# A planned attention stage: copies out of shared PSUM banks enter the operation order, fewer and larger loads, one longer warming

## The chip, the cores and the metric

One core of one Trainium2 chip. The metric is the device time of one execution in microseconds; the median of three executions stands for the kernel.

## The reference

Causal attention with a forget bias on 4 batches of 8 heads (576 positions, head size 64, float32), and behind it two feed-forward blocks on the 2304 x 512 result. Per head, `c` is the running sum of `max(s, 0)` and

```
scores = q @ k.T / 8 + min(c[j] - c[i], 0)      (j > i: -1e9)
attn   = exp(scores - rowmax);  attn /= sum(attn) + 1e-9;  x = attn @ v
x = (sigmoid(x @ w_gate) * (x @ w_val)) @ w_out        (512 -> 1536 -> 512)
h = x @ w_in;  out = (h * cos(h)) @ w_out2             (512 -> 2048 -> 512)
```

The weights arrive as 64-bit floats and are decoded on the chip into a high and a low float32 part; a product of the blocks takes three matmuls (high x high, high x low, low x high).

## The kernel before, in words

The attention works on 16 pairs of heads. Its operations carry short names with the pair's number last. For pair p: `GQ`, `GK` load Q and K (512 of the 576 rows, one DMA per head; the last 64 rows of all 8 heads of a batch come by `GQT`, `GKT`), `GV` loads V (one DMA per head with all 576 rows, the fifth chunk filled up with 64 rows of the next head), `DB` spreads the running sums over the partitions (pair 0 does it with matmuls `B0`, `B1` instead, and copies `BC`), `PQ`, `PK` transpose Q and K with TensorE, `HQ`, `HK` copy them out of PSUM, `A4`, `A5`, `A3`, `A2`, `A0` are the score matmuls of the query blocks, `ZT`, `ZA`, `ZM`, `Z` mask the bias on GpSimd, `X` is the biased row minimum on VectorE (L662), `E` the exponential on ScalarE (L666), `T` the transposes of the weights back into PSUM (L444), `C` their copies into the SBUF tile `pt` (L433 on ScalarE, L437 on VectorE), `V0`, `V1` the product with V (L736, L738), `U` its copy to `w`, and `RA RC RT RR RD RB M XH XL` form the reciprocals of the sums (RA on GpSimd L745, RC on VectorE L748), turn them, store them to DRAM (RD), spread them back into `rb` (RB, L762), multiply (`M`, L768) and split the result in high and low parts.

The two `T` of one query-block group (blocks 0 and 1, or the two heads of block 2 or of block 3) write into one pair of PSUM banks, and two `C` copies empty it. Where these two copies go to different engines, the program makes the second wait for the first, since both read the same banks.

The order of all this is a list, `SEQ`, of about 1,100 names (the suffix `:a`, `:d` or `:p` gives ScalarE, VectorE or GpSimd). Every engine, and SyncE that issues the loads, works through its own part of the list strictly in order. `Plan.run` goes through the list with planned durations only to hand out buffers and PSUM banks. The list was made outside the kernel with the same plan. Behind the attention, `I0` to `I7` are the first up-projection of the first feed-forward block, and from `moe()` on the blocks follow; `glu` (L835 to L844) is their first gate, on ScalarE and VectorE.

At the start TensorE runs six matmuls on zeros (L453), six 256-column matmuls as warming (`warm0`, L495), `B0` and `B1` on 32 rows (L569), the first transposes (L552), and six more warming matmuls (`warm1`) ahead of the first scores (L626, L631).

Of the kernel before, what the change touches and what calls it, by code (L numbers as in the profile page):

```python
# [10 lines left out]
F32 = mybir.dt.float32  # L11
# [72 lines left out]
class Op:  # L84
    __slots__ = ("name", "alts", "fn", "deps", "ready", "bufs", "out", "unit", "start", "end", "n", "xfer", "mode")
# [5 lines left out]
SWITCH = 0.15  # L91


class Plan:
# [3 lines left out]
    def op(self, name, alts, rd=(), wr=(), needs=(), xfer=0.0, at=0.0):  # L98
        o = Op()
        o.name, o.alts, o.xfer = name, alts, xfer  # L100
# [25 lines left out]
    def run(self, seq):  # L126
# [3 lines left out]
        for word in seq.split():  # L130
# [32 lines left out]
WARM = 2  # L163
# [31 lines left out]
C1.2.8:d E1.1.9 w0mant_hi E0.1.9 A2.9 E1.3.9 U7:d Z0.10:p C0.4.8:a T0.1.9 RB6 T0.0.9 C0.0.9:a RC8 A5.9 ZM0.3.10 T0.3.9 T1.3.9 C0.1.9:a GK13 X0.2.9 GV8 X1.2.9 Z1.10:p
E1.2.9 C1.3.9:a X0.4.9 PQ11 ZT1.10 PK11 ZT0.10 A3.10 ZM1.3.10 GQT12 ZA1.10 ZA0.10 HK11:a C0.3.9:d HQ11:d GQ12 A4.10 RT8 A0.10 E0.4.9 M6:p X1.3.10 XH5:p X0.3.10 RR8:a
# [23 lines left out]
def kernel(  # L220
# [14 lines left out]
    B, H, S, D = q.shape  # L235
# [153 lines left out]
    def attention():  # L389
        with ExitStack() as c2:  # L390
# [79 lines left out]
            def setup_tail(u):  # L470
# [6 lines left out]
                for i in range(NV):  # L477
                    u.memset(VN[i][TAIL:P, NT4], 0.0)
# [592 lines left out]
```

## Time and profile before

| | us |
|---|---|
| median of 3 executions | 1038.0 |
| lowest, highest | 1037.33, 1042.3 |
| the profiled execution | 1042.41 |
| its span (first to last instruction) | 1040.6 |
| TensorE busy in it | 1014.0 |
| VectorE, ScalarE, GpSimd busy | 704.6, 477.9, 410.4 |

Busy times are sums over instructions; TensorE's are modelled, so that a stretch that is called busy is not one at its peak. Idle times stand in brackets behind an instruction with what ended them.

### The profile page before, as it was taken

Reading aid. Unit: us, or ns where it says so; the run is one execution under the profiler, and the core shown is the slowest. Engines: PE = TensorE matmul, PEld = TensorE weight load, DVE = VectorE, ACT = ScalarE, POOL = GpSimd, SP = SyncE. Lnnn points to the kernel's source line nnn. Section 1 sums busy time; section 2 is a strip of 40 time slices with the busy share of each in tenths; the row PEclk is TensorE's granted clock in tenths of the full one; section 3 lists DMA queues with packets and bytes.
Section 4 is the critical chain, followed back from the end, with each engine's and each line's share of the span. In section 5 each row is a group of like instructions: output and inputs, shape, how many; then the busy total and the mean of one; then the engine's idle time right before and its main releaser. Section 6 shows DMA issues by size and latency. Waiting matters only on the chain.

```text
span 1040.6 us, 17428 instructions
## 1 busy us (share of the span) xinstructions
PE 1014.0 (97%) x6554; PEld 917.6 (88%) x6554; DVE 704.6 (68%) x1366; ACT 477.9 (46%) x1079; POOL 410.4 (39%) x489
## 2 busy tenths in 40 slices
PE   9999897899999999999999999999999999999998
PEld 5665555799999999999999999999999999999997
DVE  5777875565655557644334888888688878886565
ACT  5888885342222222222121335666555455554443
POOL 4456885341222223321111234555255535552222
PEclk9999999999999999999999999999999999999999
DMA  7778763221111112111010112122011201200111
GB/s 175 182 183 194 186 156 81 93 82 41 41 41 41 61 42 61 62 43 39 21 42 21 41 61 61 41 61 61 1 61 42 60 22 41 62 1 13 49 61 61
DMA packets 93956, 69.94 MB, mean 67 GB/s; under 512 B 61296, under 2 KB 82160, under 8 KB 93872
## 3 DMA queue, kind: packets, MB, share of 16 engines
q1 hardware_dynamic: 92224, 68.37, 23.1%
q8 instruction: 51, 0.84, 0.3%
q10 hardware_dynamic: 1648, 0.47, 0.2%
q14 instruction: 33, 0.27, 0.1%
HBM read 63.95 MB, written 4.87 MB: 66 GB/s over the span
## 4 chain that ended last, share of the span: by engine, by line
PE 81%; DVE 0%; ACT 0%; issue 0%; DVEq 0%; ACTq 0%
PE pw L356 21%; PE pw L357 21%; PE pw L355 21%; PE pw L918 6%; PE pw L919 6%; PE pw L920 6%; DVE acc L936 0%; DVE gl L844 0%; ACT gh L838 0%; ACT tm L835 0%; DVEq L1066 0%; ACTq L838 0%
## 5 line engine op out<-in xcount | busy, mean ns | idle before, releaser
L355 PE MATMUL pw<-XH,wp 128*128 128x384 f32 x960 | 323.1, 337 | 1.0 <-DVE w L437 1.0
L356 PE MATMUL pw<-XL,wp 128*128 128x384 f32 x960 | 323.0, 336 | 0.0
L357 PE MATMUL pw<-XH,wp 128*128 128x384 f32 x960 | 322.9, 336 | 0.0
L310 POOL TENSOR_TENSOR wp<-wm,wp 128x512 fp32r<-128x512 f32 x68 | 101.4, 1491 | 228.6 <-DVE wp L309 228.0
L355 PEld LDWEIGHTS pw<-XH,wp 128*128 128x128 f32 x960 | 180.4, 188 | 4.8 <-DVE w L437 1.1
L356 PEld LDWEIGHTS pw<-XL,wp 128*128 128x128 f32 x960 | 180.3, 188 | 3.6
L357 PEld LDWEIGHTS pw<-XH,wp 128*128 128x128 f32 x960 | 180.3, 188 | 0.0
L908 POOL TENSOR_TENSOR gl<-tm,gh 128x384 fp32r<-128x384 f32 x96 | 108.9, 1135 | 142.7 <-ACT gh L907 142.6
L302 POOL TENSOR_TENSOR wm<-wm,wx 128x512 int32<-128x512 int32 x68 | 90.5, 1331 | 181.8 <-DVE wm L301 177.3
L836 DVE TENSOR_TENSOR tm<-pw,tm 128x384 f32<-128x384 f32 x72 | 40.1, 557 | 154.2 <-PE pw L357 139.6
L918 PE MATMUL pw<-wp,gh 128*128 128x512 f32 x288 | 112.2, 389 | 0.0
L919 PE MATMUL pw<-wp,gh 128*128 128x512 f32 x288 | 112.1, 389 | 0.0
L920 PE MATMUL pw<-wp,gl 128*128 128x512 f32 x288 | 112.0, 389 | 0.0
L838 ACT CAST gh<-tm 128x384 fp32r<-128x384 f32 x72 | 37.0, 514 | 140.7 <-DVE tm L836 139.9
L893 DVE SCALAR_TENSOR_TENSOR tm<-tm 128x384 f32<-128x384 int32 x96 | 99.1, 1032 | 3.3
L894 ACT ACTIVATE tm<-tm 128x384 f32<-128x384 f32 x96 | 50.5, 527 | 108.9 <-DVE tm L893 108.9
L355 PE MATMUL pw<-gh,wp 128*128 128x384 f32 x288 | 97.0, 337 | 2.3 <-ACT gh L838 2.3
L356 PE MATMUL pw<-gl,wp 128*128 128x384 f32 x288 | 97.3, 338 | 0.2 <-DVE gl L844 0.2
L357 PE MATMUL pw<-gh,wp 128*128 128x384 f32 x288 | 96.7, 336 | 0.0
L289 ACT ACTIVATE wx<-wx,ebias 128x512 int32<-128x512 int32 x68 | 49.2, 723 | 100.3 <-DVE wx L288 99.3
L666 ACT ACTIVATE pu<-pu,nm 128x576 f32<-128x576 f32 (+4 forms) x144 | 83.3, 581 | 5.4 <-DVE nm L662 5.4
L901 DVE SCALAR_TENSOR_TENSOR tm<-tm,pw 128x384 f32<-128x384 f32 x96 | 52.8, 550 | 42.4 <-ACT tm L895 42.4
(100 smaller groups left out, 1621.4 us busy)
## 6 DMA issues: line engine op xcount, KB each, us to landing
raw<-in_moe_w_out_dram SPq DMA_DIRECT2D x28, 512.0 KB
CB<-cum_d SPq DMA_DIRECT2D x15, 576.0 KB
raw<-in_moe_w_in_dram SPq DMA_DIRECT2D x16, 512.0 KB
raw<-in_moe_w_gate_dram SPq DMA_DIRECT2D x12, 512.0 KB
raw<-in_moe_w_val_dram SPq DMA_DIRECT2D x12, 512.0 KB
VN<-in_v_dram SPq DMA_DIRECT2D x31, 160.0 KB
rb<-rec_d SPq DMA_DIRECT2D x32, 144.0 KB
out_dram<-acc SPq DMA_DIRECT2D x17, 256.0 KB
```

What stands on the lines that cost most here:

```text
L302: pool.tensor_tensor(m, m, st["x"], ALU.add)
L310: pool.tensor_tensor(w[:, 1], m, f(w[:, 0]), ALU.subtract)
L355: pe.matmul(ps, wh, xh, start=first, stop=False)
L356: pe.matmul(ps, wh, xl, start=False, stop=False)
L357: pe.matmul(ps, wl, xh, start=False, stop=last)
L666: act.activation(o, o, AF.Exp, bias=NMT[nm.slot][:, col:col + 1], scale=-1.0, accum_out=SUMS[sums.slot][:, col:col + 1])
L893: dve.scalar_tensor_tensor(r, kk, -TWO_PI_LO, r, ALU.mult, ALU.add)
L901: dve.scalar_tensor_tensor(g, r, -0.5, h, ALU.add, ALU.mult)
L908: pool.tensor_tensor(gl, g, f(gh), ALU.subtract)
L918: pe.matmul(ps, gh[:, ts], w[:, 0], start=it["first"], stop=False)
L919: pe.matmul(ps, gh[:, ts], w[:, 1], start=False, stop=False)
L920: pe.matmul(ps, gl[:, ts], w[:, 0], start=False, stop=it["last"])
```

## The change

The list is new as a whole. The plan that goes with it knows that a copy waits for all transposes and copies ahead of it in its banks; some planned durations differ. Q and K of a pair come in one DMA each, V's fifth chunk comes once per batch into a tile of its own (`vt`), the warming is one operation of 11 matmuls and `warm1` is gone, and `B0`, `B1` read all 128 rows of a tile that VectorE has set to zero first.

```diff
-    def op(self, name, alts, rd=(), wr=(), needs=(), xfer=0.0, at=0.0):
+    def op(self, name, alts, rd=(), wr=(), needs=(), xfer=0.0, at=0.0, ser=None):
...
+            if o.ser:
+                b, copy = o.ser
+                s = max(s, b.turned if copy else 0.0, b.copied + LAT[b.unit] if b.unit not in (None, u) else 0.0)
...
-WARM = 2
+WARM = 11
...
-tail cum GQ0 warm0 GKT0 B1 B0 GQT0 PQ0 table GK0 out BC0:a BC1:a GQ1 ZT0.0 PK0 GK1 warm1 Z0.0:p HQ0:a ZT1.0 Z1.0:p DB1 ZM0.3.0 PQ1 ZA0.0 HK0:d A3.0 ZM1.3.0 ZA1.0 X0.3.0
...
-X1.1.14 E0.3.14 T0.4.13 X1.0.14 V0.12 X0.0.14 X0.1.14 E0.2.13 E1.0.14 E1.1.14 XL9:p RC12 DB15 V1.12 M11:p E0.1.14 C0.4.13:d RT12 A2.14 U12:d RA13 E0.0.14 RR12:a ZM0.2.14
-E1.3.14 T0.1.14 RC13 ZT0.15 RD12 X0.2.14 T0.0.14 Z0.15:p C0.0.14:d XL10:p T0.2.13 C0.1.14:a Z1.15:p T1.2.13 A5.14 E0.2.14 T0.3.14 X1.2.14 RB12 ZM0.3.15 T1.3.14 X0.4.14
...
-w2split U14:a C0.4.15:d V0.15 XH13:d M14:d RD15 XH14:d XL14:p RB15 V1.15 U15:d XL13:d M15:p XH15:a XL15:p
+warm0 GQ0 tail cum table GKT0 GK0 GQT0 B0 BC0:d PK0 PQ0 Z0.0:p B1 out HQ0:a BC1:a ZT0.0 GK1 HK0:d A4.0 ZA0.0 GQ1 A0.0 X0.1.0 Z1.0:a PK1 DB1 ZT1.0 A3.0 GQ2 ZA1.0 X0.0.0
...
+X1.0.15 E0.2.14 RD12 E0.1.15 M11:d XH11:p E0.0.15 E1.0.15 T0.1.14 E1.1.15 U13:d T0.0.14 C0.0.14:a A5.14 ZM0.3.15 RB12 T0.1.15 RA13 T0.0.15 X0.4.14 C0.1.14:a w1split A5.15
...
+T0.4.14 T0.4.15 XH12:p C0.4.15:d RB13 XL12:p w2exponent I5 I6 RC15 I7 XL11:d RD14 T0.2.15 M13:d C0.4.14:a w2mant_hi RT15 T1.2.15 C0.3.15:a C0.2.15:a V0.14 w2mant_lo
+RR15:a V1.14 U14:d RD15 w2sign RB14 C1.2.15:a M14:d RB15 w2split V0.15 XH13:p XL13:p V1.15 XH14:a U15:d M15:d XL14:p XH15:d XL15:d
...
-            VN = [att.tile([P, NQ, 2, D], F32, name=f"VN{i}") for i in range(NV)]
+            VN = [att.tile([P, NT4, 2, D], F32, name=f"VN{i}") for i in range(NV)]
+            VT = [att.tile([P, PB, 2, D], F32, name=f"vt{i}") for i in range(2)]
...
+            dve.memset(WT[1], 0.0)
...
-            for i in range(WARM):
+            for i in range(1):
...
-                    for z in range(6):
-                        pe.matmul(PW[:, wm.slot, 0:2 * P], one_b[:, 0:P], one_b, start=z == 0, stop=z == 5)
...
+                    for z in range(WARM):
+                        pe.matmul(PW[:, wm.slot, 0:2 * P], one_b[:, 0:P], one_b, start=z == 0, stop=z == WARM - 1)
...
-                        for e in range(2):
-                            u.dma_start(out=QKN[x][qk.slot][:, :, e], in_=src[e, 0:NT4 * P].rearrange("(p c) d -> p c d", c=NT4))
+                        u.dma_start(out=QKN[x][qk.slot], in_=src[:, 0:NT4 * P].rearrange("e (p c) d -> p c e d", c=NT4))
...
-                                pe.matmul(PW[:, bs.slot + z, 0:HS], ident[0:NH, e:e + 1].to_broadcast([NH, P]), cs[:, z * HS:(z + 1) * HS], start=True, stop=True)
+                                pe.matmul(PW[:, bs.slot + z, 0:HS], ident[:, e:e + 1].to_broadcast([P, P]), WT[1][:, z * HS:(z + 1) * HS], start=True, stop=True)
...
+                        u.dma_start(out=VN[vn.slot][:, :, e], in_=v[b, 2 * j + e, 0:NT4 * P].rearrange("(c p) d -> p c d", p=P))
+                add(f"GV{p}", {"sp": 1.1}, load_v, rd=[], wr=[vn], xfer=1.2)
...
+                        u.dma_start(out=VT[vt.slot][0:TAIL].rearrange("p i e d -> p (i e) d"), in_=v[b, :, NT4 * P:S].rearrange("h p d -> p h d"))
...
-                if p == 0:
-                    add("warm1", "pe:700", warm1[0], rd=[("turned", x) for x in "QK"], wr=[warm1[1], "go"])
...
+                            add(f"T{e}.{t}.{p}", f"pe:{tT}", transp, rd=[pu, *[(pu, z) for z in es], *src], wr=[(tps, t, e), ("t01", p, t)], needs=[pt], ser=(tps, 0))
+                            add(f"C{e}.{t}.{p}", f"act:{tH} dve:{tD}", pt_copy, rd=[(tps, t, e), "tail"], wr=[(pt, z, t) for z in es], ser=(tps, 1))
```

## Rows read from the trace of the kernel before

**Rows 1.** Busy time by stretch: stretch, length; PE, PEld, DVE, ACT, POOL; clock, DMA, GB/s.

```profile
31.00:164.30 133.30, 120.09 (x1532) 75.55 (x1530) 98.25 (x317) 112.72 (x336) 89.90 (x199) 0.99 0.69 176
194.00:1040.60 846.60, 842.66 (x4559) 808.30 (x4559) 572.02 (x954) 332.68 (x658) 292.45 (x226) 1.00 0.15 46
```

**Rows 2.** Timeline of the start: start, length, engine, line, operation, count.

```profile
1.21 0.54 DVE L455 MEMSET pu<- 32x576 f32 x1
1.21 2.74 PE L453 MATMUL pw<-pu 128*128 128x512 bf16 x6 [1.21 <-DVE pu L451]
...
3.75 1.49 PE L495 MATMUL pw<-ident 128*128 128x256 bf16 x6
5.16 4.20 PE L569 MATMUL pw<-w,ident 32*128 32x288 f32 x8
...
9.89 0.64 PE L552 MATMUL pw<-ident,Kn 64*128 64x64 f32 x8
...
12.55 1.83 PE L626 MATMUL pw<-K,Q 64*128 64x512 f32 x4
...
14.21 0.41 PE L552 MATMUL pw<-ident,Kn 64*128 64x64 f32 x8
...
14.53 0.69 DVE L662 CUSTOM_DVE_ANT_0 pu<-pw,CB 128x512 f32<-128x512 f32 x1 [3.01 <-PE pw L626]
...
15.06 0.82 PE L626 MATMUL pw<-K,Q 64*128 64x128 f32 x8
```

**Rows 3.** Waits of ScalarE, VectorE, TensorE, 14 to 187 us: total, times, longest.

```profile
ACT pt L433 <- DVE pt L437: 9.0, 9, 3.6
...
DVE pt L437 <- ACT pt L433: 4.4, 4, 2.0
...
PE pw L444 <- ACT pt L433: 6.4, 8, 3.5
...
PE pw L738 <- DVE pt L437: 1.7, 1, 1.7
...
PE pw L626 <- ACT pt L433: 1.1, 2, 0.6
```

**Rows 4.** Timeline around 158 us, one chain of waits.

```profile
156.07 1.40 POOL L768 TENSOR_TENSOR w<-w,rb 128x576 f32<-128x576 f32 x1 [2.38 <-DMA rb<-rec_d]
...
157.84 0.21 DVE L748 RECIPROCAL rc<-rc 128x9 f32<-128x9 f32 x1 [2.78 <-POOL rc L745]
...
159.14 0.65 ACT L433 COPY pt<-pw 128x256 f32<-128x256 f32 x2 [3.60 <-DVE pt L437]
...
159.84 0.71 PE L444 MATMUL pw<-ident,pu 64*128 64x64 f32 x16 [3.46 <-ACT pt L433]
```

**Rows 5.** Busy time by stretch at a lower granted clock (columns as in Rows 1).

```profile
161.00:164.00 3.00, 3.00 (x18) 1.73 (x14) 1.06 (x3) 1.59 (x5) 1.81 (x7) 0.50 0.32 132
...
195.00:198.00 3.00, 3.00 (x12) 3.00 (x11) 2.49 (x5) 0.79 (x2) 0.14 (x1) 0.50 0.38 128
```

**Rows 6.** Timeline of the handover to the feed-forward block.

```profile
182.96 2.81 PE L738 MATMUL pw<-pt,VN 128*64 128x512 f32 x20 [1.66 <-DVE pt L437]
...
183.76 0.74 DVE L768 TENSOR_TENSOR w<-w,rb 128x576 f32<-128x576 f32 x1
184.54 0.46 DVE L437 CAST XH<-w 128x576 fp32r<-128x576 f32 x1
...
186.58 0.75 DVE L780 TENSOR_TENSOR XL<-w,XH 128x576 fp32r<-128x576 f32 x1
...
188.12 1.42 POOL L768 TENSOR_TENSOR w<-w,rb 128x576 f32<-128x576 f32 x1 [1.64 <-DMA rb<-rec_d]
...
189.57 0.67 ACT L433 CAST XH<-w 128x576 fp32r<-128x576 f32 x1 [7.66 <-POOL w L768]
...
193.43 0.44 PE L355 MATMUL pw<-gh,wp 128*128 128x384 f32 x1 [2.28 <-ACT gh L838]
```

**Rows 7.** K's loads: durations of an issue in ns (min/median/max), first and last start.

```profile
L521 SPq DMA_DIRECT2D Kn<-in_k_dram x32: 540/622/1577, 2.0 to 136.3; - x32
```

More of the change, by code (lines that the diff above doesn't have):

```diff
@@ L84 @@
 class Op:
-    __slots__ = ("name", "alts", "fn", "deps", "ready", "bufs", "out", "unit", "start", "end", "n", "xfer", "mode")
+    __slots__ = ("name", "alts", "fn", "deps", "ready", "bufs", "out", "unit", "start", "end", "n", "xfer", "mode", "ser")
 SAME = {"pe": 0.0}
@@ L90 @@
 MODE = {"V": 1, "warm": 2, "B": 2, "I": 2}
-SWITCH = 0.15
+SWITCH = 0.1
 class Plan:
@@ L96, in __init__ @@
         self.ops, self.writer, self.readers = [], {}, {}
-    def op(self, name, alts, rd=(), wr=(), needs=(), xfer=0.0, at=0.0):
+    def op(self, name, alts, rd=(), wr=(), needs=(), xfer=0.0, at=0.0, ser=None):
         o = Op()
+        o.ser = ser
         o.name, o.alts, o.xfer = name, alts, xfer
@@ L148, in run @@
                 o.end = free[u]
+            if o.ser:
+                b, copy = o.ser
+                if copy:
+                    b.copied, b.unit = o.end, u
+                else:
+                    b.turned = max(b.turned, o.end + LAT["pe"])
             for b in o.bufs:
@@ new lines @@
+X1.2.2 T0.3.2 GQ7 T1.3.2 C0.1.2:a ZM1.3.3 GV3 RT1 DB4 X0.3.3 GK5 V0.1 E0.4.2 X1.3.3 ZM1.2.3 ZA0.3 V1.1 ZA1.3 RR1:d M0:d PK4 ZM0.2.3 C1.3.2:d C0.3.2:d T0.4.2 E0.3.3 HK4:d
+E1.3.3 U1:a E0.2.2 Z1.4:p PQ4 A4.3 HQ4:d ZT1.4 C0.4.2:a A0.3 X1.0.3 E1.2.2 XH0:p A2.3 Z0.4:p T0.2.2 X0.1.3 E1.0.3 E0.1.3 ZA1.4 X0.0.3 X1.1.3 T1.2.2 X1.2.3 ZM1.3.4 X0.2.3
+T0.3.3 E0.0.3 T1.3.3 E1.1.3 T0.0.3 GV2 ZT0.4 C1.2.2:a ZA0.4 C1.3.3:d ZM0.3.4 C0.2.2:a E0.2.3 C0.3.3:d T0.1.3 A5.3 A3.4 GQT8 GQ5 RD1 X0.4.3 PQ5 RA2 C0.1.3:a C0.0.3:a A4.4
@@ L421, in attention, with add @@
             DMA = {"sp": 0.62}
-            def add(name, alts, fn, rd=(), wr=(), needs=(), xfer=0.0, at=0.0):
+            def add(name, alts, fn, rd=(), wr=(), needs=(), xfer=0.0, at=0.0, ser=None):
                 if isinstance(alts, str):
@@ L426, in add @@
                     alts = {u: float(t) / 1000 for u, t in alts.items()}
-                o = plan.op(name, alts, rd, wr, needs, xfer, at)
+                o = plan.op(name, alts, rd, wr, needs, xfer, at, ser)
                 o.fn = lambda: fn(units[o.unit])
@@ L476, in setup_tail @@
                     u.memset(PU[4][i][:, S:NQ * P], 0.0)
-                for i in range(NV):
-                    u.memset(VN[i][TAIL:P, NT4], 0.0)
+                for i in range(2):
+                    u.memset(VT[i][TAIL:P], 0.0)
             add("cum", "dve:1850", setup_cum, wr=["cum"], at=2.85)
@@ L737, in pv @@
                             for e in range(2):
-                                pe.matmul(o[half(e), x0:S], VN[vn.slot][:, c, e], PT[pt.slot][:, e, c * PST + x0:c * PST + S], start=c == 0, stop=c == NQ - 1)
-                    add(f"V{g}.{p}", f"pe:{sum((1040, 720, 520, 320, 260)[c] for c in cs_)}", pv, rd=[vn, *[(pt, e, t) for e in range(2) for t in range(cs_[0], NQ)]] + ([ov] if g else [("v", p - 1)]), wr=[ov] if g else [ov, ("v", p)])
+                                pe.matmul(o[half(e), x0:S], VN[vn.slot][:, c, e] if c < NT4 else VT[vt.slot][:, j, e], PT[pt.slot][:, e, c * PST + x0:c * PST + S], start=c == 0, stop=c == NQ - 1)
+                    add(f"V{g}.{p}", f"pe:{sum((1050, 728, 470, 320, 210)[c] for c in cs_)}", pv, rd=[vn, vt, *[(pt, e, t) for e in range(2) for t in range(cs_[0], NQ)]] + ([ov] if g else [("v", p - 1)]), wr=[ov] if g else [ov, ("v", p)])
                 w, rc, rr, rb, rt = Buf(pl["w"]), Buf(pl["rc"]), Buf(pl["rr"]), Buf(pl["rb"]), Buf(pl["pw"], 2)
```

120 lines of the change are left out of this document (55 added, 65 removed).

## The prediction

> **What bounds the kernel now.** I read the stretches first. From 194 us to the end TensorE is busy 842.66 of 846.60 us with the feed-forward blocks [rows 1]; the change touches nothing there, so at most the first 194 us are open. In the middle of the attention, 133.30 us long, TensorE is called busy 120.09 us, ScalarE 112.72, VectorE 98.25 [rows 1]. No engine is full: each works in the list's order and they wait for one another. Half a per cent, about what a measurement of this kernel can tell from no change, is 5.2 us; it has to come out of waits within those 194 us. So the waits come next, and then the timeline where they are long.
>
> [...] **Copies wait for copies:** ScalarE stood 9.0 us behind a copy of VectorE's, VectorE 4.4 us behind one of ScalarE's, and TensorE's transposes 6.4 us behind ScalarE's copies [rows 3]. The longest is a chain [rows 4]: GpSimd's M11 waited 2.38 us for `rb`, worked 1.40 us, RA13 came behind it, VectorE waited 2.78 us for that with RC13, its copy C0.0.14 stood behind RC13, ScalarE's C0.1.14 waited 3.60 us for that copy, and TensorE 3.46 us. [...] **The handover:** `XH15` stands last on ScalarE; it waited 7.66 us for M15, only then the table load and the gate could follow, and TensorE waited 2.28 us for the gate's result [rows 6].
>
> **The sum.** It is made against the profiled execution, 1042.41 us, which is 4.4 us above the median of 1038.0.
>
> Start. VectorE's new clearing of a 576-column tile costs about the 0.54 us of the memset of that width [rows 2] and stands ahead of the matmuls on zeros: these move from 1.21 to about 1.75 us and end at 4.3 us. Eleven warming matmuls at 1.41/6 = 0.235 us (from 3.75 to 5.16 for six) end at 6.9 us. B0 alone is four instructions of 4.20/8 = 0.525 us, so 9.0 us at the pace of the trace. The pace there was the low one: eight of K's transposes took 0.64 us at 9.89 and 0.41 at 14.21 [rows 2]. At the high one B0 ends at 7.9 us. PK0 and PQ0 then take 1.3 us at the low pace and 0.8 at the high (an estimate from the two rows of K's transposes), and B1, which stands ahead of A4.0 and covers the copies HQ0 and HK0, 2.1 or 1.05: the first scores begin at 9.8 to 12.4 us instead of 12.55. Ahead of them `warm1` and PQ1 are gone. The first reduction follows A4.0 and A0.0 instead of a 1.83 us A3.0; A0 took 0.82 us at the high pace [rows 2] and A4 is about as long, so some 1.6 us, or twice that: the reduction comes at 11.4 us, or at 15.6, instead of 14.53 [rows 2]. That is a gain of 3.1 us or a loss of 1.1. What lies between is the clock; as TensorE has hardly a gap from 1.75 us on, I take a value nearer the gain, **2.0**.
>
> On the clock here the rows say that the work before 14 us ran at the low pace though TensorE had hardly a gap. [...]
>
> Copies. Counted in the two lists, pairs of copies that empty one pair of banks on two engines fall from 28 to 14, and transposes placed behind the first copy of their own banks from 6 to 1. The chain of rows 4 loses its links: M11 moves to VectorE, C0.0.14 and C0.1.14 both go to ScalarE. It is worth its 3.46 us and half of the 3.0 us at half clock, 1.5 [rows 4, 5]: **5.0**. Of TensorE's other waits behind copies, 6.4 - 3.46 = 2.9 and 1.1 us [rows 3], half goes with half the splits: **2.0**. The ends are nothing and 4.0. A list that is new as a whole also brings waits of its own; below as a rival.
>
> Tail. V0.15 waited 1.66 us for VectorE's C0.4.15, which stood behind the weights' `w2split` [rows 6]. It now stands well ahead of it, but V0.15 still needs C1.2.15, a few names before it: **0.8**, between 0 and 1.66. At the handover M15, XH15 and XL15 are now on VectorE: 0.74 + 0.46 + 0.75 = 1.95 us after `rb` lands [rows 6], and ScalarE's table load no longer stands behind XH15. `rb` landed at 188.12 us in the trace; with the gate's multiply and cast, some 1.2 us, TensorE could go on at 191.3 to 191.9 instead of 193.43: **1.6**, between 0 and 2.28. If the wait shrinks so, the low clock behind it goes too, half of 3.0 us [rows 5]: **1.5**, or nothing. Ahead of it U15 comes before M15 on VectorE, so the bank that the gate's matmuls wait for is not delayed by `rb`.
>
> Loads. Q and K drop 32 issues of 0.62 us [rows 7], about 20 us of SyncE's time; V goes from 33 issues to 36 with the four `GVT`, about 2 us more. Behind SyncE's queue stand RD, RB and DB. I cost this at nothing by itself: SyncE issues ahead of need, and the one visible price of a late `rb` is in the chain already counted. If that cover goes (a load three names ahead of its use, as GQ5 before PQ5), the next wait is TensorE's for Q. Bytes and pieces hardly change. The fifth V chunk is the same matmul from another tile; `ser` and the new durations cost nothing on the chip.
>
> Together 2.0 + 5.0 + 2.0 + 0.8 + 1.6 + 1.5 = 12.9 us, hence 1042.4 - 12.9 = 1029.5. I do not take the 4.4 us to the median off once more: they are about the size of the one chain of rows 4, and the executions from 1037.33 to 1042.3 may differ by just that. **1029.5 us.**
>
> **The rivals.** First, the whole middle gets quicker: ScalarE and VectorE waited 9.0 + 4.4 us for each other's copies, 9.8 without the chain [rows 3, 4]; half of it, 4.9 us, reaches the end on top, and the median stands below the profile as before. That gives 1029.5 - 4.9 - 4.4 = 1020. For it: ScalarE is the fullest engine behind TensorE [rows 1]. Against it: 20 us of ScalarE's middle were idle anyway, so its time is not what bounds the pace everywhere.
>
> Second, the middle gains nothing: the waits go from copies to masks, reductions and loads. Then the start and the tail remain, 2.0 + 3.9: 1036.5, within half a per cent of 1038. For it: the chain of rows 4 began with a late `rb`, not with a copy, and such chains can form anywhere in a list. Against it: the splits are halved.
>
> Third, on the other side: **M on VectorE waits for `rb`.** The new list puts five M on VectorE instead of one, and M13, M14 and M15 follow their RB by 10, 2 and 8 names, with the last weights' decode, U14 and U15 behind them. A wait like GpSimd's 2.38 us [rows 4] then stops VectorE itself. Where TensorE is out of work behind it, the price is 3.46 us and 1.5 for the clock; three of them take back 15 us: 1044.5. It decides from the point where `rb` lands about 1 us after M's turn. Against it: V0 and V1 of the last pairs, 2.81 us each and more [rows 6], cover TensorE there, and no copy on VectorE stands behind M13 in the list.
>
> Fourth, the change may not do what it says at the start, where the lower clock stays: 1029.5 + 3.1 = 1032.6, still inside the first forecast.
>
> **How the numbers follow.** Forecast 0.45 (1023 to 1032.8), quicker middle 0.20, start and tail only 0.23, M's stalls 0.12. The first two are faster by over 0.5% (below 1032.8 us): 0.65; the third is no change: 0.23; the last slower: 0.12. The range for 8 in 10 leaves out most of the stalls and the far end of the quick middle: 1018 to 1040.
>
> **What would show it.** Right: the first reduction before 13.5 us; fewer and shorter waits of ScalarE behind VectorE's copies and the other way; no TensorE wait over 3 us in the middle, and no stretch at 0.50; TensorE waiting under 1 us for the gate; the feed-forward part as long as before, 846 us, and beginning near 181 us. Wrong: a first reduction at 14 us; VectorE waiting for `rb` ahead of M13 to M15 with TensorE idle; copies waiting as long as before; a feed-forward part of another length, on which all of this would say nothing.

## The result and the profile after

The changed kernel takes 1025.91 us (median of 4 executions, 1024.72 to 1028.06), the kernel before in the same series 1039.65 (4 executions, 1037.33 to 1042.3). The ratio is 0.9869, 95% interval 0.9837 to 0.9902: faster by 1.3%. The profiled execution took 1028.06 us with a span of 1026.3; TensorE is called busy for 1007.6 us of it, VectorE 709.7, ScalarE 475.3, GpSimd 411.2.

The sum came out, its parts did not. Read from the two timelines, stage by stage (us; the first V product marks where a pair is finished, so 0 to 13 is the steady middle):

| stage | before | after | gain |
|---|---|---|---|
| span's start to first reduction | 14.53 | 11.64 | 2.9 |
| first reduction to V0.0 | 16.44 | 14.44 | 2.0 |
| V0.0 to V0.13 | 133.36 | 120.21 | 13.2 |
| V0.13 to V0.15 | 16.67 | 18.61 | -1.9 |
| V0.15 to the first down product | 12.43 | 16.60 | -4.2 |
| first down product to the span's end | 847.2 | 844.8 | 2.4 |
| sum | 1040.6 | 1026.3 | 14.3 |

(V0.13 starts at 164.33 before and at 146.29 after, the down product at 193.43 [rows 6] and 181.50.) Two pairs of these rows belong together. The new list puts some work behind V0.13 that stood ahead of it: the middle holds 1506 matmuls instead of 1532 [rows 1], the stretch from V0.13 to V0.15 holds 196 instead of 158, and its -1.9 is that work (busy time by stretch, columns as in [rows 1], kernel before, then kernel after):

```profile
164.33:181.00 16.67, 14.85 (x158) 10.35 (x158) 9.86 (x30) 10.39 (x29) 7.24 (x9) 1.00 0.34 75
146.29:164.90 18.61, 17.00 (x196) 11.95 (x196) 14.06 (x37) 14.41 (x46) 10.45 (x14) 1.00 0.36 90
```

Together the middle and this stretch gain 11.3 us, where 7.8 was forecast (5.0, 2.0 and 0.8). The last two rows belong together because the lower clock moved from one into the other (V0.15 to the down product, kernel before, then kernel after):

```profile
181.00:193.43 12.43, 7.54 (x55) 5.62 (x51) 5.97 (x9) 3.60 (x5) 6.40 (x5) 1.00 0.12 31
164.90:181.50 16.60, 10.97 (x54) 9.00 (x51) 8.06 (x13) 3.32 (x5) 5.95 (x5) 0.69 0.33 99
```

The same matmuls are busy 3.4 us longer there at a granted clock of 0.69, and behind the down product, where the kernel before has its 3 us at 0.50 [rows 5], the kernel after has 1.00 (181.5 to 185 us). Together these two rows lose 1.8 us, where a gain of 3.1 was forecast. Lines of the trace after are numbered a little higher: the copies are L445 and L449, the transposes L456, the reduction L670, `V0` L744, `rb` L770, `M` L776, `XL` L788, the gate L843 to L852, a weight fetch L295.

The start, timeline of the kernel after:

```profile
4.36 2.55 PE L508 MATMUL pw<-ident 128*128 128x256 bf16 x11
6.71 1.41 PE L577 MATMUL pw<-w,ident 128*128 128x288 f32 x4
8.05 0.46 PE L560 MATMUL pw<-ident,Kn 64*128 64x64 f32 x8
...
11.64 0.42 DVE L670 CUSTOM_DVE_ANT_1 pu<-pw,CB 128x256 f32<-128x256 f32 x1 [2.00 <-PE pw L634]
```

B0's four instructions take 0.35 us each where the trace before had 0.525, and K's first eight transposes take 0.46 us at 8.05 instead of 0.64 at 9.89 [rows 2]: the high pace is there before the first operand is turned.

The middle: busy time by stretch (columns as in [rows 1]), V0.0 to V0.13 of the kernel after.

```profile
26.10:146.30 120.20, 115.50 (x1506) 75.37 (x1504) 96.79 (x307) 107.38 (x325) 87.50 (x195) 1.00 0.73 188
```

Against [rows 1] TensorE's idle time falls from 13.2 to 4.7 us; its busy time falls by 4.6 more. The 3.0 us at 0.50 of [rows 5] can be 1.5 of that at most (an estimate, half of them), and 2.2 us more are busy behind V0.13 (17.00 against 14.85 above), so a good part of the 4.6 is moved work and no gain. The copies' waits, 14 to 160 us of the kernel after (total, times, longest):

```profile
ACT pt L445 <- DVE pt L449: 0.4, 2, 0.2
DVE pt L449 <- ACT pt L445: 0.6, 1, 0.6
```

In the same window the kernel before has 8.8 and 2.5 us (9.0 and 4.4 up to 187 us [rows 3]); 0.4 and 0.6 are left. No wait of TensorE behind a copy into `pt` is among the kernel after's waits there; TensorE's longest group is 1.3 us in two waits behind an exponential. That looks as if the forecast had named the cause; the experiments say otherwise.

The handover, timeline of the kernel after, all engines:

```profile
164.12 7.00 SPq L770 DMA_DIRECT2D rb<-rec_d  x4
...
169.25 0.76 DVE L776 TENSOR_TENSOR w<-w,rb 128x576 f32<-128x576 f32 x1 [2.68 <-DMA rb<-rec_d]
...
170.04 0.67 ACT L445 CAST XH<-w 128x576 fp32r<-128x576 f32 x1 [6.94 <-DVE w L776]
170.73 1.28 ACT L843 ACT_TABLE_LOAD   x1
172.03 0.49 ACT L843 ACTIVATE tm<-pw 128x384 f32<-128x384 f32 x1
...
172.57 0.69 PE L366 MATMUL pw<-XH,wp 128*128 128x384 f32 x1 [4.79 <-ACT tm L843]
...
173.89 1.91 DVE L776 TENSOR_TENSOR w<-w,rb 128x576 f32<-128x576 f32 x1 [2.88 <-DMA rb<-rec_d]
...
176.33 0.76 DVE L788 TENSOR_TENSOR XL<-w,XH 128x576 fp32r<-128x576 f32 x1
...
177.61 0.69 PE L366 MATMUL pw<-XH,wp 128*128 128x384 f32 x1 [0.83 <-DVE tm L844]
...
181.50 0.34 PE L366 MATMUL pw<-gh,wp 128*128 128x384 f32 x1
```

M14 waits 2.68 us for `rb` and M15 2.88, both on VectorE; ScalarE's XH14 waits 6.94 us for M14 with the gate's table load behind it; TensorE stands 4.79 us behind the sigmoid, 0.83 behind the gate's multiply, which stands behind XL15 on VectorE, and the granted clock is 0.50 in between (busy time by stretch, kernel after):

```profile
172.00:176.00 4.00, 3.43 (x11) 3.43 (x12) 2.07 (x2) 0.51 (x2) 3.11 (x3) 0.50 0.17 45
176.00:180.00 4.00, 3.17 (x10) 2.66 (x9) 2.08 (x4) 0.51 (x1) 0.00 (x0) 0.50 0.40 131
```

### The profile page after: what moved, and what is told of

The parts are those of the page before. It is cut to its first block, busy times and chain, and to the rows that moved or that the text cites. A ratio compares the mean times of both kernels' runs of the same rounds, so it can differ in the third digit from the quotient of the medians.

```text
span 1026.3 us, 17410 instructions
## 1 busy us (share of the span) xinstructions
PE 1007.6 (98%) x6553; PEld 918.4 (89%) x6553; DVE 709.7 (69%) x1365; ACT 475.3 (46%) x1081; POOL 411.2 (40%) x489
## 4 chain that ended last, share of the span: by engine, by line
PE 90%; DVE 2%; DMA 2%; POOL 2%; ACT 2%; issue 1%; SPq 1%; DVEq 0%; POOLq 0%; ACTq 0%
PE pw L366 21%; PE pw L367 21%; PE pw L368 21%; PE pw L926 6%; PE pw L927 6%; PE pw L928 6%; PE pw L634 2%; DMA rb<-rec_d 2%; PE pw L746 1%; PE pw L456 1%; DVE pu L670 1%; ACT pu L674 1%; PE pw L639 1%; PE pw L560 1%; DMA Qn<-in_q_dram 1%
## 5 line engine op out<-in xcount | busy, mean ns | idle before, releaser
L674 ACT ACTIVATE pu<-pu,nm 128x128 f32<-128x128 f32 (+4 forms) x144 | 82.9, 579 | 4.7 <-DVE nm L670 4.4
```

The lines of the kernel that those rows point to most:

```text
L674: act.activation(o, o, AF.Exp, bias=NMT[nm.slot][:, col:col + 1], scale=-1.0, accum_out=SUMS[sums.slot][:, col:col + 1])
```

## The experiments

Three questions: what made the middle quicker, what the loads and the warming are worth, and what the handover waits for. Medians of different series are set against the kernel before in each, by ratio; where intervals overlap, the place in the trace is what decides. How far single executions of one list differ is seen in the kernel after and the six kernels of the handover below that keep its list up to there: V0.0 to V0.13 takes 119.1 to 121.2 us in their profiles.

### The middle

**All of the change without its list.** The kernel after with the list of before (`warm1` taken out, each `GVT` behind the first `GV` of its batch); warming, loads, `B0` and the plan stay as changed.

```diff
-warm0 GQ0 tail cum table GKT0 GK0 GQT0 B0 BC0:d PK0 PQ0 Z0.0:p B1 out HQ0:a BC1:a ZT0.0 GK1 HK0:d A4.0 ZA0.0 GQ1 A0.0 X0.1.0 Z1.0:a PK1 DB1 ZT1.0 A3.0 GQ2 ZA1.0 X0.0.0
+tail cum GQ0 warm0 GKT0 B1 B0 GQT0 PQ0 table GK0 out BC0:a BC1:a GQ1 ZT0.0 PK0 GK1 Z0.0:p HQ0:a ZT1.0 Z1.0:p DB1 ZM0.3.0 PQ1 ZA0.0 HK0:d A3.0 ZM1.3.0 ZA1.0 X0.3.0
...
```

> The changed kernel (new loads, vt, warming, cast on 128 rows) with the operation order of before; warm1 taken out, GVT put behind GV0, GV4, GV8, GV12. Theory (the order carries the middle, and loads are hidden): only the start's 2 to 3 us come, 1033 to 1037. Rival (SyncE's shorter queue is what made the middle quicker): more than half of the gain, 1025 to 1031.

1039.16 us, ratio 0.9991 (0.9972 to 1.0009): nothing is left. Waits from 14 to 160 us of this kernel, and its chain at 158 us in the timeline:

```profile
ACT pt L445 <- DVE pt L449: 8.6, 8, 3.2
...
PE pw L456 <- ACT pt L445: 5.5, 6, 3.1
...
157.96 1.12 PE L456 MATMUL pw<-ident,pu 64*128 64x64 f32 x16 [3.06 <-ACT pt L445]
```

The waits of [rows 3] and the chain of [rows 4] are back. The start is still quicker (first reduction 12.05, V0.0 2.5 us earlier than before), but V0.13 is only 1.1 us earlier and the down product 0.5. Under the old order an early start is used up on the way.

**The number of split pairs, from both sides.** A pair of copies that empties one pair of banks is called split when the two go to different engines, and joined when both go to one. In the kernel after, the second copy of 14 joined pairs goes to the other engine, which makes 28 split pairs again; in the kernel before, all 28 are joined, 14 on each engine. One line of each:

```diff
-C0.3.6:d X1.3.7 E1.2.6 X0.3.7 RA6 V0.5 E0.0.7 V1.5 PK8 C1.3.6:d RB4 E1.1.7 T0.1.7 ZM0.2.7 w0exponent E1.0.7 RC6 T0.0.7 A5.7 E0.3.7 GK9 U5:a T0.4.6 C0.1.7:a HK8:d X0.4.7
+C0.3.6:d X1.3.7 E1.2.6 X0.3.7 RA6 V0.5 E0.0.7 V1.5 PK8 C1.3.6:a RB4 E1.1.7 T0.1.7 ZM0.2.7 w0exponent E1.0.7 RC6 T0.0.7 A5.7 E0.3.7 GK9 U5:a T0.4.6 C0.1.7:a HK8:d X0.4.7
...
-X0.4.3 PK4 GV3 PQ4 RA2 Z1.4:p A2.3 PQ5 E1.3.3 HK4:d HQ4:a T0.3.3 RD1 A4.4 X1.2.3 ZT0.4 E0.4.3 X0.2.3 T1.3.3 C0.3.3:d HQ5:a PK5 HK5:d A0.4 C1.3.3:a RC2 E1.2.3 ZM0.3.4
+X0.4.3 PK4 GV3 PQ4 RA2 Z1.4:p A2.3 PQ5 E1.3.3 HK4:d HQ4:a T0.3.3 RD1 A4.4 X1.2.3 ZT0.4 E0.4.3 X0.2.3 T1.3.3 C0.3.3:d HQ5:a PK5 HK5:d A0.4 C1.3.3:d RC2 E1.2.3 ZM0.3.4
```

> The changed kernel with the second copy of 14 pairs (blocks 1 to 3) moved to the other engine, so that 28 pairs are split as before; the copies' total time on each engine stays about the same. Theory (copies that share banks on two engines wait for each other and TensorE behind them): half of the middle's gain goes, 1029 to 1034. Rival (what counts is that the order knows where its copies wait, not how many are split; a copy or two more out of place are absorbed): within 2 us, 1024 to 1028.

> The kernel before with both copies of every pair of banks on one engine (28 pairs joined, 14 on each side, so that each engine has as many copies as before; ScalarE gets 0.17 us more in all). Theory of the prediction (copies that wait for copies hold TensorE): 13 us of engine waits go, and 2 to 6 us of the time, 1033 to 1037 beside 1039. Rival (as the split of the new order cost next to nothing, joining gains nothing, and an order made without it may even lose): 1037 to 1041.

After with 28 splits: 1027.41 us, 0.9877 (0.9856 to 0.9898). Its waits from 14 to 160 us:

```profile
ACT pt L445 <- DVE pt L449: 4.4, 4, 2.8
...
DVE pt L449 <- ACT pt L445: 1.7, 5, 0.6
```

About half of the copies' waits are back, and the middle takes 121.2 us, inside the spread of after's own list. Before with no split: 1042.27 us, 1.0019 (0.9999 to 1.0039). No copy waits for a copy, and still (waits from 14 to 165 us, and the timeline at 162.84 us):

```profile
PE pw L444 <- DVE pt L437: 4.7, 4, 3.1
...
162.84 0.71 PE L444 MATMUL pw<-ident,pu 64*128 64x64 f32 x16 [3.07 <-DVE pt L437]
```

TensorE's stop at about 160 us is there as before, behind the one engine that now has both copies; V0.13 comes 3.0 us later (in the longest of its twelve executions, 1045.16 us). In both kernels the waits of copies for copies show how late an engine is; putting them in or taking them away made no difference that shows in the time. The prediction's other count, transposes placed behind the first copy of their own banks, stays at 6 in this kernel and at 1 in the one with 28 splits: no run changes it alone.

**The chain of rows 4 alone.** M11 goes behind RA13 on GpSimd, so that RA13, RC13 and both copies no longer wait for `rb`.

```diff
-X1.1.14 E0.3.14 T0.4.13 X1.0.14 V0.12 X0.0.14 X0.1.14 E0.2.13 E1.0.14 E1.1.14 XL9:p RC12 DB15 V1.12 M11:p E0.1.14 C0.4.13:d RT12 A2.14 U12:d RA13 E0.0.14 RR12:a ZM0.2.14
+X1.1.14 E0.3.14 T0.4.13 X1.0.14 V0.12 X0.0.14 X0.1.14 E0.2.13 E1.0.14 E1.1.14 XL9:p RC12 DB15 V1.12 E0.1.14 C0.4.13:d RT12 A2.14 U12:d RA13 M11:p E0.0.14 RR12:a ZM0.2.14
```

> The kernel before with M11 behind RA13 on GpSimd, nothing else: RC13 and the copy behind it on VectorE no longer stand behind M11's wait for rb. Theory of the prediction (the chain near 158 us costs its wait and the low clock behind it, 5.0 us): V0.13 begins some 4 to 5 us earlier, 1033 to 1036. Rival (the handover's time is set by the last rb and XL15, so V0.13 begins earlier and the feed-forward block does not, or less than half as much): 1036.5 to 1040.

1040.39 us, 1.0014 (0.9997 to 1.0031). The same stop in its timeline:

```profile
159.09 0.71 PE L444 MATMUL pw<-ident,pu 64*128 64x64 f32 x16 [1.82 <-ACT pt L433]
```

3.46 us became 1.82, V0.13 comes 1.2 us earlier, the down product 0.7, and the median shows nothing. At most about a quarter of the 5.0 us counted for the chain came back, and 1.2 us is less than the profiles of one list differ (2.1 us, above).

### The loads and the warming

Both are undone under the new list: Q and K with one DMA per head; six warming matmuls, `B0` and `B1` on 32 rows, no clearing.

```diff
-                        u.dma_start(out=QKN[x][qk.slot], in_=src[:, 0:NT4 * P].rearrange("e (p c) d -> p c e d", c=NT4))
+                        for e in range(2):
+                            u.dma_start(out=QKN[x][qk.slot][:, :, e], in_=src[e, 0:NT4 * P].rearrange("(p c) d -> p c d", c=NT4))
```

> The changed kernel with Q and K again in one DMA per head, 32 more issues of some 0.62 us on SyncE. Theory (the issues are hidden): within 2 us of the changed kernel, 1024 to 1028. Rival (SyncE's queue delays RD, RB and DB, and the order was made for the shorter one): 1030 to 1036.

```diff
-WARM = 11
+WARM = 6
...
-            dve.memset(WT[1], 0.0)
...
-                                pe.matmul(PW[:, bs.slot + z, 0:HS], ident[:, e:e + 1].to_broadcast([P, P]), WT[1][:, z * HS:(z + 1) * HS], start=True, stop=True)
+                                pe.matmul(PW[:, bs.slot + z, 0:HS], ident[0:NH, e:e + 1].to_broadcast([NH, P]), cs[:, z * HS:(z + 1) * HS], start=True, stop=True)
```

> The changed kernel with 6 warming matmuls instead of 11, the running sums cast on 32 rows as before, and without the clearing of the tile. Theory (the longer warming and the full rows bring the high clock before B0, which showed in B0's 1.41 us for four instructions instead of 2.1): B0, B1 and the first transposes run at the low level again, the first reduction comes near 14 us instead of 11.6, and 2 to 5 us are lost: 1028 to 1031. Rival (the clock rises when it will, and the middle's waits absorb the start): within 1.5 us, 1024.5 to 1027.5.

**Loads:** 1029.46 us, 0.9903 (0.988 to 0.9926), 3.5 us above after; the intervals overlap, but the place is plain. V0.13 comes at 150.48, 4.2 us later than after, though the start was 1.0 us earlier; V0.0 to V0.13 takes 125.4 us, outside the 119.1 to 121.2 of after's list. Timeline of the kernel with separate loads, then the same operations of the kernel after:

```profile
90.45 1.20 SPq L771 DMA_DIRECT2D rb<-rec_d  x2
...
95.69 1.42 POOL L777 TENSOR_TENSOR w<-w,rb 128x576 f32<-128x576 f32 x1 [4.67 <-DMA rb<-rec_d]
...
101.56 3.36 PE L635 MATMUL pw<-K,Q 64*128 64x128 f32 x12 [3.37 <-DVE nm L671]
```

```profile
89.05 1.20 SPq L770 DMA_DIRECT2D rb<-rec_d  x2
...
93.69 1.41 POOL L776 TENSOR_TENSOR w<-w,rb 128x576 f32<-128x576 f32 x1 [2.10 <-DMA rb<-rec_d]
```

Ahead of this `rb` SyncE issues Qn, Kn and Qn twice each instead of once, and `rb` goes out 1.4 us later. GpSimd waits 4.67 us instead of 2.10, its next mask comes at 99.28 us instead of 97.63, VectorE's reduction behind it at 99.61 instead of 97.96 with a wait of 2.57 us, and TensorE stands 3.37 us where after stood 0.97. Behind that the granted clock of the kernel with separate loads is 0.50 (by stretch):

```profile
101.50:106.00 4.50, 4.44 (x20) 2.14 (x22) 2.01 (x12) 2.15 (x10) 3.37 (x6) 0.50 0.77 210
```

**Warming:** 1028.67 us, 0.989 (0.9867 to 0.9913), above after by 2.8 us of the medians and 2.2 by the ratios; the intervals overlap, so a loss is likely but not clear of the noise. Its start, by stretch:

```profile
10.00:13.00 3.00, 3.00 (x23) 2.31 (x24) 0.01 (x1) 1.25 (x2) 1.27 (x5) 0.50 1.05 280
```

The granted clock is 0.59 from 8 to 10 us, ahead of the first scores (10.14 us), and 0.50 from 10 to 13, where all ten kernels with eleven warming matmuls have 1.00. The first reduction comes 1.35 us later, V0.0 2.5 and V0.13 3.3. The same few microseconds that the old order swallowed reach the end of the middle under the new one. K's first transposes still ran at the high pace here (0.46 us at 7.35, behind a wait of 1.03 us for the load); the pace fell behind them, and `B1` took 2.09 us at 8.12 instead of 1.24. Three kernels with eleven matmuls waited 0.25 to 0.62 us for the same load and kept the pace (`B1` 1.24 us). The run changes the number of matmuls, the rows of `B0` and `B1` and the clearing together, and which of them keeps the pace is not separated.

### The handover

**Other banks for the first gate.** In the kernel after, the banks of the first gate are the ones that `I0` to `I7` fill; here it starts at bank 2.

```diff
-    turn = [0, 0, 0]
+    turn = [2, 0, 0]
```

> The changed kernel with one number changed: the first feed-forward block's matmuls begin in banks 2 and 3 instead of 0 and 1, where the first gate's sums (I0 to I7) lie in the new plan. Theory (the gate of block 1 stands 4.8 us because it waits for the sigmoid to empty its bank): the gate's matmuls start at about 168 us instead of 172.6 and end near 172; the down product then waits for VectorE's multiply, which stands behind M15 until about 177, so it starts near 178.3 instead of 181.5: some 3 us faster, 1022 to 1025. Rival (the 4.8 us are a wait for VectorE's U15 or for weights, the bank only comes last): no gain, 1026.

1025.52 us, 0.988 (0.9861 to 0.9898): no gain that shows. TensorE no longer waits for the sigmoid; the wait goes whole to the next step of the same path (timeline):

```profile
178.02 0.69 PE L366 MATMUL pw<-gh,wp 128*128 128x384 f32 x1 [5.65 <-ACT gh L846]
```

**XH14 off ScalarE**, so that the table load need not wait for M14.

```diff
-RR15:a V1.14 U14:d RD15 w2sign RB14 C1.2.15:a M14:d RB15 w2split V0.15 XH13:p XL13:p V1.15 XH14:a U15:d M15:d XL14:p XH15:d XL15:d
+RR15:a V1.14 U14:d RD15 w2sign RB14 C1.2.15:a M14:d RB15 w2split V0.15 XH13:p XL13:p V1.15 XH14:p U15:d M15:d XL14:p XH15:d XL15:d
```

> The changed kernel with XH14 on GpSimd instead of ScalarE. Theory (banks and VectorE's M15 hold the handover, ScalarE's late table load is only one link): the sigmoid comes at about 165 us instead of 172.0, the gate's first half starts at 168, but its second half still waits for VectorE's multiply behind M15 near 177: within 1.5 us of the changed kernel, 1024.5 to 1027. Rival (XH14 on ScalarE, which waits 6.9 us for M14, is the cause): the whole wait of 4.8 us and the low clock behind it go, 1017 to 1020.

1026.42 us, 0.9886 (0.9867 to 0.9905): no gain. The sigmoid now waits 6.81 us for the weights' last split on GpSimd, and TensorE 3.98 us for the sigmoid.

**M14 and M15 off VectorE.** M, XH and XL of the last two pairs go to GpSimd behind the weights' split; then the same with the other banks as well.

```diff
-RR15:a V1.14 U14:d RD15 w2sign RB14 C1.2.15:a M14:d RB15 w2split V0.15 XH13:p XL13:p V1.15 XH14:a U15:d M15:d XL14:p XH15:d XL15:d
+RR15:a V1.14 U14:d RD15 w2sign RB14 C1.2.15:a w2split M14:p RB15 V0.15 XH13:p XL13:p V1.15 XH14:p U15:d XL14:p M15:p XH15:p XL15:p
```

> The changed kernel with M14, XH14, M15, XH15, XL15 on GpSimd and w2split ahead of M14; banks as they are. Theory (my third rival did happen in the tail: VectorE and, through XH14, ScalarE stood behind M's wait for rb): sigmoid near 165, multiply near 168.6, so the gate runs from 168 to 172 without a wait and without the low clock; the feed-forward's down product starts near 172.5 instead of 181.5: 1016 to 1019. Rival (the handover waits for the weights' last piece or for banks): less than 3 us faster, 1023 to 1026.

> As the kernel with M14, XH14, M15, XH15, XL15 on GpSimd, and the feed-forward's matmuls begin in banks 2 and 3. Theory (with VectorE and ScalarE free the bank is emptied before the gate needs it): the same within 1 us, 1016 to 1018. Rival (the bank alone costs): 1 to 3 us faster than with the banks unchanged.

1029.22 us (0.991, 0.9891 to 0.9929) and 1028.61 us (0.9904, 0.9887 to 0.9921): both medians above after's, though VectorE no longer waits for `rb`. (From V0.15 to the end of the span their profiles take 861.9 and 862.1 us; the kernel after takes 861.4, and the three other kernels with its last line of the list 858.5 to 859.4. What in that stretch makes them slower is not shown.) Timeline of the first:

```profile
167.80 0.49 ACT L843 ACTIVATE tm<-pw 128x384 f32<-128x384 f32 x1 [5.41 <-POOL wp L321]
...
175.58 1.40 POOL L788 TENSOR_TENSOR XL<-w,XH 128x576 fp32r<-128x576 f32 x1
...
177.01 0.51 ACT L846 CAST gh<-tm 128x384 fp32r<-128x384 f32 x1 [8.72 <-POOL XL L788]
```

This line named what had been missing: the sigmoid is done at 168.3, and the gate's next tile, `gh`, waits 8.72 us for **XL15**, with which it has no data in common. `gh` comes from a pool that is laid on the attention's memory, and XL15 is that memory's last user. In the kernel after, the weights' next fetch waits for the same end (waits of SyncE, 160 to 180 us, kernel after):

```profile
SPq L295 <- DVE XL L788: 6.0, 1, 6.0
```

**The first gate on memory of its own.** To the last kernel a pool is added that is open from the start, for the first sigmoid's result, `gh` and `gl`; the gate's rings behind it get one buffer fewer.

```diff
+            head = c2.enter_context(tc.tile_pool(name="head", bufs=1))
+            sg0 = head.tile([P, TB], F32, name="sg0")
+            gh0 = head.tile([P, TB], F32R, name="gh0")
+            gl0 = head.tile([P, TB], F32R, name="gl0")
...
-            gp = c2.enter_context(tc.tile_pool(name="gp", bufs=4))
+            gp = c2.enter_context(tc.tile_pool(name="gp", bufs=3))
...
-                gh = gp.tile([P, TB], F32R, name="gh")
+                gh = gh0 if it is items1[0] else gp.tile([P, TB], F32R, name="gh")
```

> The changed kernel with M14 to XL15 on GpSimd and the feed-forward's first banks 2 and 3, and the first gate's three SBUF tiles in a small pool of their own, which lies where the weights' first pieces were decoded instead of on the attention's memory (tm has 4 slots, gp 3 buffers, in exchange). Theory (the first gate's tile gh lies on memory of the attention's pool and so waits for XL15, the last instruction that uses that pool; that is why neither banks nor engines mattered): the down product starts at 172 to 173 us instead of 178 to 181.5, no low clock behind it, perhaps 1 to 2 us of wait at the second gate: 1017 to 1022. Rival (gh waits for something else at the end of GpSimd's queue, as the weights): as before that edit, 1026 to 1029.

1031.52 us, 0.993 (0.9907 to 0.9952): the slowest of these. Timeline:

```profile
171.93 0.34 PE L366 MATMUL pw<-gh,wp 128*128 128x384 f32 x1
...
177.77 1.44 POOL L788 TENSOR_TENSOR XL<-w,XH 128x576 fp32r<-128x576 f32 x1
179.23 0.37 SPq L295 DMA_DIRECT2D raw<-in_moe_w_gate_dram  x1
...
183.89 0.72 ACT L300 ACTIVATE wx<-wx,ebias 128x512 int32<-128x512 int32 x1 [12.50 <-DVE wx L299]
...
186.52 0.47 ACT L847 ACTIVATE tm<-pw 128x384 f32<-128x384 f32 x1
...
188.60 0.66 PE L366 MATMUL pw<-gh,wp 128*128 128x384 f32 x1 [10.04 <-issue]
```

The down product starts at 171.93 us, where the kernel it was made from had 178.91 behind a wait of 7.40 for `gh`: the tile was on the attention's memory. But the next fetch still waits for XL15 and goes out at 179.23; its decode stands ahead of the second gate's sigmoid in ScalarE's order, and TensorE is idle 10.04 us. (The profile names no releaser for that wait; the fetch, its decode and the sigmoid follow one another on the lines above.) XL15's end is the gate, whichever tile waits for it.

**XL15 earlier.** XL15 ends two trips of reciprocals: RB14, M14, RB15, M15. In the kernel after, SyncE's four `rb` issues take 7.00 us from the first to the last, because RB15 fills the one `rb` that M14 still has to read. Here RB15 goes into a tile of the `CB` kind that is free by then, RB14 and RB15 are issued one behind the other, both M follow the last U, XH14 goes to GpSimd, XH13 and XL13 come a line earlier in the list, and the first gate starts at bank 2.

```diff
-RR15:a V1.14 U14:d RD15 w2sign RB14 C1.2.15:a M14:d RB15 w2split V0.15 XH13:p XL13:p V1.15 XH14:a U15:d M15:d XL14:p XH15:d XL15:d
+RR15:a V1.14 w2sign U14:d RD15 RB14 RB15 C1.2.15:a w2split V0.15 V1.15 U15:d M14:d XH14:p M15:d XL14:p XH15:d XL15:d
...
-    turn = [0, 0, 0]
+    turn = [2, 0, 0]
...
-                        u.dma_start(out=RBT[half(e)], in_=rec_d[p, e].unsqueeze(0).to_broadcast([64, S]))
+                        u.dma_start(out=(RBT if p < NP - 1 else CB[rb.slot][:, 0, 0:S])[half(e)], in_=rec_d[p, e].unsqueeze(0).to_broadcast([64, S]))
...
-                    u.tensor_tensor(WT[w.slot], WT[w.slot], RBT, ALU.mult)
+                    u.tensor_tensor(WT[w.slot], WT[w.slot], RBT if p < NP - 1 else CB[rb.slot][:, 0, 0:S], ALU.mult)
```

> The changed kernel with a second place for the last pair's reciprocals (the load of RB15 goes into a tile of the CB kind that is free by then, so that it need not wait for M14's last read of the one rb buffer), RB14 and RB15 issued one behind the other, XL14 and the two M on VectorE after the last U, and banks 2 and 3 for the first gate block. Theory (the handover is set by the end of XL15, and that by two round trips of reciprocals one behind the other): RB15 lands near 171 us instead of 173.9, XL15 ends near 173 instead of 177.1, the first down product starts at 174 to 175 instead of 181.5, and the median is 1019 to 1023 us. Rival (the handover waits for something else, the landing of the reciprocals themselves or the sigmoid's chain): the down product stays within 3 us of 181.5, and the median is 1025 to 1028 us.

**1022.76 us** (5 executions, 1021.34 to 1023.43), 0.9844 (0.9824 to 0.9863). Timeline:

```profile
164.35 1.13 SPq L770 DMA_DIRECT2D rb<-rec_d  x2
165.57 1.17 SPq L770 DMA_DIRECT2D CB<-rec_d  x2
...
168.79 1.32 DVE L776 TENSOR_TENSOR w<-w,rb 128x576 f32<-128x576 f32 x1
170.04 0.75 DVE L776 TENSOR_TENSOR w<-w,CB 128x576 f32<-128x576 f32 x1
...
171.66 1.88 DVE L788 TENSOR_TENSOR XL<-w,XH 128x576 fp32r<-128x576 f32 x1
...
174.72 0.45 PE L366 MATMUL pw<-gh,wp 128*128 128x384 f32 x1 [2.33 <-ACT gh L846]
```

Neither M waits, XL15 ends at 173.54 instead of 177.09, the down product starts at 174.72 instead of 181.50, and the fetch goes out 3.5 us earlier. This is the fastest of all kernels here, 3.2 us below after, and 2.8 below the kernel that has only the other banks, by medians of different series. Its interval overlaps both of theirs; what is shown beyond the medians is that the place moved as the theory said. Of the 6.8 us at the down product 4.7 reach the end of the span. A part of both belongs to the one execution of after that was profiled: from V0.15 to the end of the span this kernel takes 856.5 us, 4.9 less than after and 2.0 less than the shortest (858.5) of the three other kernels with after's last line. The run changes the buffer, the order and the banks together. What the second place itself does is in the lines: M15 begins at 170.04, where in the kernel after RB15 was only then issued.

## Why the prediction was right and where it failed

**Right:** 1029.5 forecast, 1025.91 measured, inside the first forecast's own range; profile against profile the gain is 1042.41 - 1028.06 = 14.4 us, where the sum said 12.9. The feed-forward part came out at 844.8 us, no half-clock stretch and no stop over 1 us is left in the middle (granted clock 1.00, longest stop of TensorE 0.97 us), and the first reduction is before 13.5. That the sum came within 1.5 us of the profile is in part luck: the terms of the middle were too small, those of the handover had the wrong sign, and the two errors offset each other.

**Start, 2.0:** measured 2.9 at the first reduction (2.8 to 3.8 in the eight kernels with after's start), near the 3.1 of the better end, and 4.9 at V0.0, with 12 matmuls fewer between the two. The step was right. The sum let it pass to the end without a question; under the old list the same early start left 0.5 us at the down product, under the new one its loss costs 2.8 us in the median, not clear of the noise. The eleven matmuls begin at 4.36 us and take 2.55 us in the kernel after, 0.23 each, and 1.50 us, 0.14 each, in the kernel with 28 splits (below); `B0` behind them begins between 5.70 and 6.71 us in the ten kernels that have them, so the pace rises within them in some and at or behind their end in others.

```profile
4.36 1.50 PE L508 MATMUL pw<-ident 128*128 128x256 bf16 x11
```

In all ten the pace had risen before the first transposes, eight of which take 0.46 or 0.47 us, and the first reduction came between 10.68 and 12.05. That is one profile of each, so a later rise in another execution is not excluded.

**Copies, 5.0 + 2.0:** this is the step that failed, though it erred on the low side (with V0.15's 0.8 it promised 7.8 us up to V0.15, and 11.3 came). The chain of rows 4, counted at 3.46 + 1.5, gave at most 1.2 us at V0.13 and nothing in the median when it was taken away by itself. The 2.0 for fewer split pairs has no support: joining all 28 made the old order no faster, splitting 28 in the new one left its middle at 121.2 us, inside its spread. What the runs showed in place of these terms is the order as a whole: the same operations with the old list lose all of the gain. Which of its many moves carry it stays open; the runs say only that neither the splits nor that chain does when it is changed alone. The new list without both the loads and the warming was not run; taken back one at a time they cost 3.5 and 2.8 us in the median. The second rival, that new waits would replace those removed, had the mechanism of the single experiments right and the new list wrong; the first, the quicker middle, had the size.

**Loads, nothing:** wrong under the new order. "SyncE issues ahead of need" did not hold for RB, which stands in SyncE's queue behind the loads: separate loads send one `rb` out 1.4 us later, and that ends as a stop of 3.37 us with a granted clock of 0.50 behind it, 3.5 us in the median.

**Tail, 0.8 + 1.6 + 1.5:** the first came, since V0.15 no longer waits for a copy. The handover did not: forecast 1.6 us shorter up to the down product, it was 4.2 us longer in the profiled execution, 3.4 of them slower matmuls (10.97 us busy against 7.54, at a granted clock of 0.69 against 1.00). The 1.5 for the clock behind the down product came (that part took 2.4 us less), but the stretch at 0.50 now stood ahead of it, from 172 to 180 us. The step freed ScalarE's table load from XH15 and overlooked that XH14 still stands ahead of it and waits for M14, 6.94 us. The third rival's place and sign were right: M14 and M15 stopped VectorE for 2.68 and 2.88 us, and TensorE stood 4.79 us with a granted clock of 0.50 behind. Its mechanism was only half right. Moving M to GpSimd took the waits from VectorE and gained nothing; the two serial trips through one `rb` and the memory that XL15 holds were what counted. The step counted 1.95 us of work behind `rb` and 1.2 for the gate, but took the landing of M15's `rb` from the trace before, where M14 had not waited; it cannot land before M14 has read the one buffer.

The price of this place also varies with the landing of `rb`. The kernel with 28 splits has the same last line of the list; from its timeline:

```profile
168.12 0.82 DVE L776 TENSOR_TENSOR w<-w,rb 128x576 f32<-128x576 f32 x1 [1.21 <-DMA rb<-rec_d]
...
172.51 0.87 DVE L776 TENSOR_TENSOR w<-w,rb 128x576 f32<-128x576 f32 x1 [2.56 <-DMA rb<-rec_d]
...
176.97 0.45 PE L366 MATMUL pw<-gh,wp 128*128 128x384 f32 x1 [2.52 <-ACT gh L846]
```

There M14 starts 3.65 us after RB14's issue, in the kernel after 5.13, and V0.15 to the down product is 11.7 us instead of 16.6; with separate loads it is 13.3, with the short warming 14.6. Of the 4.9 us between the first two 3.6 are the matmuls' pace: 54 of them are busy 10.97 us in the kernel after and 7.33 in the one with 28 splits, where the granted clock stayed at 1.00 up to the down product. So of the 4.2 us lost in the profiled execution a part belongs to that execution. Its 1028.06 us are also the longest of the four.

## What to carry to other kernels

A wait shows who came last, not what the time is worth: before a stop between in-order queues is counted as a gain, take it away by itself and see whether the next stage begins earlier. At the border of two phases, look for the last user of the memory on which the next phase's first tiles and fetches lie, and shorten its chain; the run with a second small buffer for the last round trip, and the moves that came with it, gained more there (1022.76 us) than any shift of work between engines (1026.42 to 1029.22). With a second place for the last `rb`, M15 begins at 170.04 us without a wait, where the kernel after waited 2.88 us and began at 173.89.

## What was not expected

- Two stops cost TensorE more than their own length: behind 4.79 us the granted clock was 0.50 from 172 to 180 us, and 54 matmuls were busy 10.97 us instead of the 7.54 for 55 before; behind 3.37 us it was 0.50 from 101.5 to 106.
- The granted clock reads 1.00 in the first 13 us of the kernel before, though K's transposes took 0.64 us at 9.89 and 0.41 at 14.21 [rows 2]. There the durations told the pace and the clock column did not; in the kernel with six warming matmuls the column showed 0.50 from 10 to 13 us.
- The same 128 x 576 split (XL) took VectorE 0.76 us alone at 176.33 and 1.88 at 171.66 in the last kernel, where GpSimd ran its own XL from 171.39; a multiply of M took 0.75 to 1.91. The slower ones overlap with GpSimd's work (the multiply of 1.91 us, at 173.89 in the kernel after, with GpSimd's two XL from 172.38 to 175.19); that one causes the other was not tried.
